# First gated units by row tile, fewer warm-up products, another order of loads, projections and reads back, in a fused spectral filter and gated feed-forward kernel

## The chip, the cores and the metric

One core of one Trainium2 chip. The time is the device time of one execution in microseconds (us); lower is better. TensorE (PE) multiplies, VectorE (DVE), ScalarE (ACT) and GpSimd (POOL) do the rest, SyncE (SP) issues most of the transfers. PEld is TensorE's weight load, which runs beside its products.

## The reference

x has 2048 rows of 512 numbers in bf16. Each row is normalised, and two branches of the result are added to x:

```python
xn = layernorm(x)                     # rows of 512, eps 1e-5
A  = irfft2(rfft2(xn) * (w_r + 1j*w_i))   # over 2048 x 512, w: 2048 x 257
g  = xn @ w_gate                      # 512 x 1792
u  = xn @ w_up                        # 512 x 1792
B  = (gelu_tanh(g) * u) @ w_down      # 1792 x 512
out = x + A + B
```

## The kernel before

The 2048 rows are 16 row tiles j of 128 rows, four of which make a block b (512 rows). Branch B is cut into units. A gated unit `geglu_unit(b, fc, a, w)` makes 128 of the 1792 hidden columns (fc is 0 to 13) for w of a block's 512 rows: four accumulating products with the gate weights into one PSUM bank, four with the up weights into another (both at line 543), gelu on ACT (L555) from the gate bank, and the product of gelu and up on DVE (L563), which frees the up bank. A projection `down_unit(b, n)` multiplies row tile n of a block with w_down in 14 products (L589), and DVE adds the result to x (L600). Row tiles have to be normalised on DVE (`ln_stats`, L411 and L412, and `ln_apply`, L434) and transposed on TensorE before branch B can use them. The inverse root of the variance comes from ACT and DVE for the first two tiles (`ln_sqrt`, `ln_recip`), from POOL for all others (`ln_rstd`).

Branch A is a two-dimensional transform cut into stages of small products: folds on POOL and DVE, `unit_A` (L616) and `unit_d` (L642) for each of 16 tiles, a shuffle through DRAM (`stage_p`), then 16 steps of `unit_B` (L691), the product with the filter on DVE (`product`) and `unit_c` (L722), whose results go to DRAM (`stage_g`, L731) and come back in another order with `back(part, pq, engine)` (L739), and last `unit_e` (L753) and `unit_fin` (L774), whose results POOL adds to x. Each of the four parts that `back` reads holds the results of four steps, in two transfers pq. `unit_B`'s result also crosses partitions through a small transfer (JX).

There is no scheduler: every engine runs its instructions in the order in which the Python code records them, with semaphore waits put in front of an instruction where it depends on another engine or on a transfer. The order is written by hand. At the start, row tiles 0 and 1 are normalised and transposed together (`transposes_by_tile`) while TensorE runs products of zeros (`warm_up`, L524; `NWARM`, of which the last 4 wait for the inverse root). Then come gated units of block 0 on the first 256 rows, fc from 0 to `NHALF`, with the statistics of tiles 2 and 3 behind the first transposes on DVE, and the same units on the other 256 rows. The rest of branch B, whole units on 512 rows, is one list of fillers; `filler(n)` takes the next n of them, and the stages of branch A call it in fixed places. At the end 15 fillers stand between `unit_e` steps, and 3 behind them.

The loads stand in SP's queue in the order of the code, but for the identity and the first up piece, which ACT issues. The weights come in five pieces of columns, `WPIECES`, the first of 384 columns (fc 0 to 2), the second of 256 (fc 3 and 4), the third of 256 (fc 5 and 6). One semaphore per piece counts gate and up together, so the first unit of a piece waits for both. PSUM has eight banks: the units at the start use six of them in turn (`ring_first`, three units), the fillers three (`ring_gu`), the projections of blocks 0 to 2 one (`ring_dn`).

Of the kernel before, what the change touches and what calls it, by code (L numbers as in the profile page):

```python
# [7 lines left out]
ACT = mybir.ActivationFunctionType  # L8
# [6 lines left out]
HD = 256  # L15
NK = 257
FF = 1792
P = 128
NJ = 16
NG = 32  # L20
NDC = 4
NFC = 14
NGG = 3
NX1 = 4
NWARM = (46, 4)
LN_EPS = 1e-5


# [123 lines left out]
class _Sched:  # L152
# [14 lines left out]
    def total(self, stream):  # L167
        return (stream, self.stream_cnt[stream])
# [59 lines left out]
def bass_parallel_sum__spectral_gfnet__glu_gated_geglu__prompt_kernel(  # L228
# [15 lines left out]
    xv = A_x.rearrange("b (p j) d -> p (b j) d", j=NJ)  # L244
# [3 lines left out]
    sch = _Sched()  # L248

    with ExitStack() as es:  # L250
# [4 lines left out]
        x_sb = sb("x_sb", [P, NJ, D])  # L255
# [63 lines left out]
        def sp_bank_bf(slot):  # L319
            return ps_bf[:, slot * 1024:(slot + 1) * 1024]  # L320
# [7 lines left out]
        ring_tr = _Ring((3, 4), bank_readers)  # L328

        streams = [("pe", 1), ("act", 1), ("dve", 1), ("pool", 1)]  # L330
        streams += [(n, 16) for n in ("x0", "x1", "x2", "x3", "xc1", "xc2", "xc3", "ident", "small", "fa", "eg", "wd", "wr", "wi",
                                      "w0", "w1", "w2", "w3", "w4", "dr0", "dr1", "perm1", "jx0", "jx1", "jx2", "jx3", "vd0_0", "vd0_1", "vd0_2", "vd1_0", "vd1_1", "vd1_2", "vd2_0", "vd2_1", "vd2_2", "vd3_0", "vd3_1", "vd3_2", "perm2", "tr2", "tr3", "out")]
        for name, inc in streams:
            sem = es.enter_context(nc.semaphore("sem_" + name))
            sch.add_stream(name, sem, inc)
# [2 lines left out]
        def load(stream, dst, src, eng="sp"):  # L338
            sch.op(eng, lambda e: e.dma_start(dst, src), stream=stream)
            return total(stream)  # L340
# [4 lines left out]
        ev_w = {}  # L345
        spec = {}

        def load_w(i, which=(0, 1), eng="sp"):
            a, b = WPIECES[i]
            for q in which:  # L350
                dst, src = ((wg_sb, B_w_gate), (wu_sb, B_w_up))[q]
                load("w%d" % i, dst[:, :, a:b], src[:, a:b].rearrange("(r p) f -> p r f", p=P), eng=eng)
            ev_w[i] = total("w%d" % i)

        def load_xc(m):
            ev = load("xc%d" % m, x_sb[:, 4 * m:4 * m + 4, :], xv[:, 4 * m:4 * m + 4, :])
# [1 line left out]
                ev_x[j] = ev  # L358

        ev_x = {}  # L360
        load_w(0, (1,), eng="act")
        for j in range(4):
            ev_x[j] = load("x%d" % j, x_sb[:, j, :], xv[:, j, :])
            if j == 1:
                load_w(0, (0,))
        load_w(1)
        load_w(2)
        load_xc(1)
        load_w(3)
# [40 lines left out]
        def ln_stats(j):  # L410
            ev = sch.op("dve", lambda e: e.bn_stats(st[:, j, :], x_sb[:, j, :]), deps=[ev_x[j]])  # L411
            ev_ag[j] = sch.op("dve", lambda e: e.bn_aggr(ag[:, j, :], st[:, j, :]), deps=[ev])  # L412
# [3 lines left out]
        def ln_sqrt(a, b):  # L416
            return sch.op("act", lambda e: e.activation(rstd[:, a:b], ag[:, a:b, 1], ACT.Sqrt, bias=eps_t[:], scale=1.0),
                          deps=[ev_ag[b - 1], ev_eps])

        def ln_recip(a, b, ev):  # L420
            ev = sch.op("dve", lambda e: e.reciprocal(rstd[:, a:b], rstd[:, a:b]), deps=[ev])
            for j in range(a, b):
                ev_rstd[j] = ev
# [9 lines left out]
        def ln_apply(j):  # L433
            ev_xn[j] = sch.op("dve", lambda e: e.tensor_scalar(xn[:, j, :], x_sb[:, j, :], ag[:, j, 0:1], rstd[:, j:j + 1],  # L434
                                                             ALU.subtract, ALU.mult), deps=[ev_rstd[j], ev_ag[j]])

        ev_xnT = {}

        def transposes_by_tile(a, b, ring):

            n = (b - a) * P
            slots = [ring.alloc(1) for _ in range(NDC)]
            banks = [sp_bank_bf(slot)[:, 0:n] for slot, _ in slots]
            evs = []
            for j in range(a, b):
                for r in range(NDC):
                    ev_t = sch.op("pe", lambda e, j=j, r=r: e.transpose(banks[r][:, (j - a) * P:(j - a + 1) * P], xn[:, j, r * P:(r + 1) * P], ident),
                                  deps=[ev_id, ev_xn[j]] + slots[r][1])
                    if j < b - 1:
                        continue  # L450
                    dst = xnT[:, r, a * P:b * P]
                    if r % 2 == 0:
                        ev = sch.op("dve", lambda e, dst=dst, r=r: e.tensor_copy(dst, banks[r]), deps=[ev_t])  # L453
                    else:
                        ev = sch.op("act", lambda e, dst=dst, r=r: e.activation(dst, banks[r], ACT.Copy), deps=[ev_t])
                    ring.add_reader(slots[r][0], ev)
                    evs.append(ev)
            for j in range(a, b):
                ev_xnT[j] = evs

        def transposes(a, b, ring, per=2):

# [66 lines left out]
        def geglu_unit(b, fc, a=0, w=512, ring=None):  # L529

            k = geg["k"]
            geg["k"] = k + 1
            s2 = k % NGG
            hb = b % 2
            ring = ring or ring_gu
            evw = [ev_w[i] for i, (lo, hi) in enumerate(WPIECES) if lo < (fc + 1) * P and fc * P < hi]
            evx = [ev_xnT[4 * b + i] for i in range(a // P, (a + w) // P)]
            gslot, gdeps = ring.alloc(1)

            def mm(e, wsb, slot, dcs=range(NDC)):  # L540
                ins = None
                for dc in dcs:
                    ins = e.matmul(gu_bank(slot)[:, 0:w], wsb[:, dc, fc * P:(fc + 1) * P], xnT[:, dc, b * 512 + a:b * 512 + a + w],  # L543
                                   start=(dc == 0), stop=(dc == NDC - 1))
                return ins

            if b == 0 and fc == 0 and a == 0:
                for dc in range(NDC):
                    ev_gm = sch.op("pe", lambda e, dc=dc: mm(e, wg_sb, gslot, (dc,)), deps=evw + [x[dc] for x in evx] + gdeps)
            else:  # L550
                ev_gm = sch.op("pe", lambda e: mm(e, wg_sb, gslot), deps=evw + evx + gdeps)
            uslot, udeps = ring.alloc(1)
            ev_um = sch.op("pe", lambda e: mm(e, wu_sb, uslot), deps=udeps)
            gg = gg_sb[s2][:, 0:w]
            ev_gg = sch.op("act", lambda e: e.activation(gg, gu_bank(gslot)[:, 0:w], ACT.Gelu_apprx_tanh),  # L555
                           deps=[ev_gm] + gg_readers[s2])
            gg_readers[s2] = []
            ring.add_reader(gslot, ev_gg)
            hdeps = []
            if fc == 0 and a == 0:  # L560
                hdeps = list(hT_readers[hb])
                hT_readers[hb] = []
            ev_h = sch.op("dve", lambda e: e.tensor_tensor(hT[hb][:, fc, a:a + w], gu_bank(uslot)[:, 0:w], gg, ALU.mult),  # L563
                          deps=[ev_um, ev_gg] + hdeps)
            ring.add_reader(uslot, ev_h)
            gg_readers[s2].append(ev_h)
            ev_h_block.setdefault(b, []).append(ev_h)
# [227 lines left out]
            finished(j, ev_o)  # L795


        NHALF = 6
        ln_stats(0)
        ln_stats(1)  # L800
        ev_sq = ln_sqrt(0, 2)
        sch.op("act", lambda e: e.activation(warm[:], eps_t[:], ACT.Gelu_apprx_tanh), deps=[ev_eps])
        ln_recip(0, 2, ev_sq)
        for n, ev in zip(NWARM, (None, ev_rstd[0])):
            warm_up(n, ev)
        ln_apply(0)
        ln_apply(1)
        transposes_by_tile(0, 2, ring_sp)
        ln_stats(2)
        ln_stats(3)  # L810
        ln_rstd(2, 4)
        for fc in range(NHALF):
            geglu_unit(0, fc, 0, 256, ring_first)
            if fc == 1:
                ln_apply(2)
                ln_apply(3)
                half_fold(0)
            if fc == 3:
                transposes(2, 4, ring_tr)
        for fc in range(NHALF):  # L820
            geglu_unit(0, fc, 256, 256, ring_first)
# [6 lines left out]
        for b in range(4):  # L828
            units = [("g", b, fc) for fc in range(NHALF if b == 0 else 0, NFC)]
            if b >= 1:  # L830
                for n, at in enumerate((4, 7, 10, 13) if b < 3 else (3, 5, 7, 14)):
                    units.insert(at + n, ("d", b - 1, n))
            fillers += units
        fillers += [("d", 3, n) for n in range(4)]
# [47 lines left out]
            negate(i)  # L882
        filler(2)
        for u in range(19):
            for v in ((14, 15) if u == 18 else (u - 4,)):
                if v >= 0:
                    unit_c(v)
            if u < 16:
                unit_B(u)
            for v in {15: (12, 13), 16: (14,), 17: (15,), 18: ()}.get(u, (u - 3,)):  # L890
                if v >= 0:
                    product(v)
            if 1 <= u < 18:
                filler()

            if u in (9, 10, 13, 14, 17, 18):
                back(u // 4 - 2, (u - 9) % 4, "act")
        for pq in range(2):
            back(3, pq, "sp")
        filler(todo["left"] - 15 - 3)  # L900
# [59 lines left out]
```

## Time and profile before

| what | value |
|---|---|
| runs | 179.92, 180.50, 180.56 us (median 180.50) |
| the profiled execution | 180.17 us, of which its span is 178.4 |
| busy: PE, DVE, ACT, POOL | 174.7, 116.0, 86.5, 55.2 us |
| PE products, gated units (L543) / projections (L589) | 117.1 / 50.7 us |
| PE's first product of zeros / first transposes / first gated product | 0.97 / 6.22 / 7.14 us |
| PE's last product ends, DVE adds it | 176.2 us, 0.29 us |
| granted TensorE clock | 1.00 in the whole span |

Busy time is a sum over all stages; each row of a timeline is: start, duration, engine, line, operation, tiles, count and, in brackets, the idle time before it and what ended that. In the chain of waits the columns are start, duration and what the chain ran through. The span is from the first to the last instruction of the program; the time has some 1.8 us more around it.

### The profile page before, as it was taken

How to read it: one execution, taken by the hardware profiler on the slowest of the kernel's cores; microseconds unless marked ns; L12 is line 12 of the kernel's file. 1: busy time of each engine (PE TensorE's matmuls, PEld its weight loads, DVE VectorE, ACT ScalarE, POOL GpSimd, SP SyncE). 2: the span in 40 equal slices, each digit the busy share in tenths (PEclk: the TensorE clock that was granted, in tenths of full speed). 3: DMA queues.
4: the chain of work that ended last, by engine and by line, in shares of the span. 5: the costliest groups of instructions: out<-in, count | busy, mean ns of one | idle time of the engine just before them, and what ended most of it. 6: DMA issues, size and time to landing. Idle time of an engine off the chain costs nothing.

```text
span 178.4 us, 3133 instructions
## 1 busy us (share of the span) xinstructions
PE 174.7 (98%) x1136; PEld 98.2 (55%) x1136; DVE 116.0 (65%) x250; ACT 86.5 (49%) x159; POOL 55.2 (31%) x54
## 2 busy tenths in 40 slices
PE   7999999999999999999999999999999999999994
PEld 7888465555555544454555555444455555555443
DVE  3768958798685628438586785954355868885731
ACT  2644357777362633066375764632173536662100
POOL 0073290373630000000000000000017869997760
PEclk9999999999999999999999999999999999999999
DMA  4999999999998693913435666744500111111101
GB/s 147 323 342 379 372 379 149 202 156 239 221 159 198 150 313 106 324 53 81 123 104 125 123 184 149 177 90 117 118 6 29 59 59 32 61 65 48 41 29 59
DMA packets 37520, 27.15 MB, mean 152 GB/s; under 512 B 6656, under 2 KB 36736, under 8 KB 37376
## 3 DMA queue, kind: packets, MB, share of 16 engines
q1 hardware_dynamic: 33664, 24.95, 55.1%
q10 hardware_dynamic: 3840, 2.00, 5.8%
q8 instruction: 9, 0.15, 0.4%
q14 instruction: 7, 0.06, 0.2%
HBM read 17.48 MB, written 6.30 MB: 133 GB/s over the span
## 4 chain that ended last, share of the span: by engine, by line
PE 87%; POOL 5%; DVE 5%; issue 1%
PE ps L543 48%; PE ps L589 25%; POOL bufC L504 5%; PE ps L524 3%; PE ps L722 2%; PE ps L753 2%; PE ps L774 2%; PE ps L691 2%; DVE bufA L434 2%; DVE hT L563 1%; PE ps L616 1%; PE ps L642 1%; PE ps L473 1%; DVE bufB L509 1%; POOL rstd L427 1%
## 5 line engine op out<-in xcount | busy, mean ns | idle before, releaser
L543 PE MATMUL ps<-xnT,wg_sb 128*128 128x512 bf16 (+1 forms) x248 | 58.5, 359 | 0.3 <-DVE xnT L453 0.3
L543 PE MATMUL ps<-xnT,wu_sb 128*128 128x512 bf16 (+1 forms) x248 | 58.6, 359 | 0.0
L563 DVE TENSOR_TENSOR hT<-ps,gg 128x512 bf16<-128x512 f32 (+1 forms) x62 | 39.3, 637 | 23.2 <-PE ps L543 21.6
L589 PE MATMUL ps<-wd_sb,hT 128*128 128x512 bf16 (+2 forms) x238 | 50.7, 367 | 0.0
L555 ACT ACTIVATE gg<-ps 128x512 bf16<-128x512 f32 (+1 forms) x62 | 34.4, 555 | 25.2 <-PE ps L543 23.6
L788 POOL TENSOR_TENSOR bufC<-bufC 128x256 bf16<-128x256 f32 x16 | 14.7, 919 | 86.5 <-DVE bufC L785 86.5
L543 PEld LDWEIGHTS ps<-xnT,wu_sb 128*128 128x128 bf16 x248 | 24.2, 98 | 24.2
L589 PEld LDWEIGHTS ps<-wd_sb,hT 128*128 128x128 bf16 x238 | 22.4, 98 | 23.2
L543 PEld LDWEIGHTS ps<-xnT,wg_sb 128*128 128x128 bf16 x248 | 23.0, 98 | 15.4 <-issue 0.5
L600 DVE TENSOR_TENSOR x_sb<-ps,x_sb 128x512 bf16<-128x512 f32 (+2 forms) x17 | 11.2, 660 | 23.9 <-PE ps L589 23.9
L792 POOL TENSOR_TENSOR x_sb<-x_sb,bufC 128x512 bf16<-128x512 bf16 x16 | 18.7, 1169 | 2.3
L504 POOL TENSOR_TENSOR bufC<-bufA 128x1024 bf16<-128x1024 bf16 x8 | 16.8, 2124 | 7.9 <-DVE bufA L434 7.9
L758 ACT ACTIVATE bufA<-ps 128x512 bf16<-128x512 f32 x16 | 9.4, 597 | 16.9 <-PE ps L753 16.9
L727 ACT ACTIVATE Vp<-ps 128x514 bf16<-128x514 f32 x16 | 9.5, 599 | 15.4 <-PE ps L722 15.4
L650 ACT ACTIVATE bufB<-ps 128x512 bf16<-128x512 f32 x16 | 11.9, 743 | 9.5 <-PE ps L642 9.5
L411 DVE BATCH_NORM_STATS2 st<-x_sb 128x6 f32<-128x512 bf16 x16 | 10.9, 678 | 2.2 <-DMA x_sb<-in_A_x_dram 2.2
L784 DVE TENSOR_TENSOR bufC<-bufC,ps 128x256 f32<-128x256 f32 x16 | 6.7, 421 | 5.3 <-ACT bufC L781 5.3
L696 ACT ACTIVATE Xc<-ps 128x514 bf16<-128x514 f32 x12 | 7.0, 595 | 1.0 <-PE ps L691 1.0
L623 ACT ACTIVATE tmp<-ps 128x512 bf16<-128x512 f32 x9 | 5.4, 597 | 4.4 <-PE ps L616 4.4
L426 POOL TENSOR_SCALAR rstd<-ag 128x4 f32<-128x4 f32 (+1 forms) x4 | 1.3, 316 | 19.9 <-DVE ag L412 19.9
L781 ACT ACTIVATE bufC<-ps 128x256 f32<-128x256 f32 x16 | 6.0, 378 | 2.6 <-PE ps L774 2.6
L788 DVE TENSOR_TENSOR bufC<-bufC 128x256 bf16<-128x256 f32 x16 | 6.8, 425 | 0.5
(50 smaller groups left out, 138.0 us busy)
## 6 DMA issues: line engine op xcount, KB each, us to landing
stage_g<-Vp SPq DMA_DIRECT2D x16, 128.5 KB, 3.1
bufC<-stage_p SPq DMA_DIRECT2D x4, 512.0 KB, 5.5
out_dram<-x_sb SPq DMA_DIRECT2D x15, 128.0 KB, 1.8
wd_sb<-in_B_w_down_dram SPq DMA_DIRECT2D x1, 1792.0 KB, 14.8
stage_p<-bufB SPq DMA_DIRECT2D x7, 256.0 KB, 5.6
wr_sb<-in_A_w_r_dram SPq DMA_DIRECT2D x6, 257.0 KB, 10.8
wi_sb<-in_A_w_i_dram SPq DMA_DIRECT2D x6, 257.0 KB, 10.0
JX<-Xc SPq DMA_DIRECT2D x24, 64.2 KB, 2.3
```

The lines of the kernel that those rows point to most:

```text
L411: ev = sch.op("dve", lambda e: e.bn_stats(st[:, j, :], x_sb[:, j, :]), deps=[ev_x[j]])
L504: ev_hf[m] = [sch.op("pool", lambda e, t=t, op=op: e.tensor_tensor(half[:, m, t, :, :], rows[:, 0, :, :], rows[:, 1, :, :], op), deps=deps ...
L543: ins = e.matmul(gu_bank(slot)[:, 0:w], wsb[:, dc, fc * P:(fc + 1) * P], xnT[:, dc, b * 512 + a:b * 512 + a + w], start=(dc == 0), stop=(d ...
L555: ev_gg = sch.op("act", lambda e: e.activation(gg, gu_bank(gslot)[:, 0:w], ACT.Gelu_apprx_tanh), deps=[ev_gm] + gg_readers[s2])
L563: ev_h = sch.op("dve", lambda e: e.tensor_tensor(hT[hb][:, fc, a:a + w], gu_bank(uslot)[:, 0:w], gg, ALU.mult), deps=[ev_um, ev_gg] + hdeps)
L589: ins = e.matmul(bank(slot)[:, 0:w], hT[hb][:, fc, jj * P:(jj + 1) * P], wd_sb[:, fc, cs], start=(fc == 0), stop=(fc == NFC - 1))
L600: ev_a = sch.op("dve", lambda e, slot=slot, cs=cs, w=w: e.tensor_tensor(x_sb[:, j, cs], bank(slot)[:, 0:w], x_sb[:, j, cs], ALU.add), deps ...
L650: ev_T[j] = sch.op("act", lambda e: e.activation(dst, src, ACT.Copy), deps=[ev_p])
L727: ev_v = sch.op("act", lambda e: e.activation(Vp[sv][:], sp_pair(slot), ACT.Copy), deps=[ev_p] + Vp_readers[sv])
L758: ev_ZT[j] = sch.op("act", lambda e: e.activation(ZT[:, :, j, :], src, ACT.Copy), deps=[ev_p] + [ev_xnT[i][0] for i in (11, 15)])
L788: y = [sch.op(("dve", "pool")[h], lambda e, h=h, op=op: e.tensor_tensor(rS[s2][:, h * HD:(h + 1) * HD], yeS[s2][:, 0, :], yeS[s2][:, 1, :] ...
L792: ev_o = sch.op("pool", lambda e: e.tensor_tensor(x_sb[:, j, :], x_sb[:, j, :], rS[s2], ALU.add), deps=[a, b, ev_xn[j]] + ev_acc.get(j, []))
```

## The change

- `NWARM` goes from (46, 4) to (38, 4).
- Gate and up of each weight piece have semaphores of their own, and the up products wait for theirs.
- SP's queue: x's tiles 0 and 1, first gate piece, second gate piece, tile 2, second up piece, tile 3. Before it was tiles 0 and 1, first gate piece, tiles 2 and 3, second gate piece, second up piece.
- Tiles 0 and 1 have a square root and a reciprocal each. Tile 0 is transposed alone, with its copies out of PSUM on DVE (`transpose_first`); the units fc 0 to 2 (`NQUARTER`) run on 128 rows of tile 0, with tile 1's transposes (copies on ACT) and tile 2's statistics behind the first of them; tile 3's statistics follow; then the same three units run on tile 1. From fc 3 on units are 256 rows wide as before.
- `NHALF` goes from 6 to 7, so the list of fillers is one unit shorter. Each place that takes a filler takes what the next place took before; in front of `unit_e` 4 are left where there were 5. The 15 between `unit_e` steps and the 3 at the end remain.
- The projections of block 2 stand among block 3's units at (1, 2, 7, 14), before at (3, 5, 7, 14). In front of `unit_e` come now unit, projection, unit, projection; before four units and one projection.
- `back` for parts 0 to 2 stands at the start of steps 10, 11, 14, 15 and twice at 17; before at the end of steps 9, 10, 13, 14, 17 and 18.

```diff
-NWARM = (46, 4)
+NWARM = (38, 4)
...
+                name = "w%d%s" % (i, "gu"[q])
+                load(name, dst[:, :, a:b], src[:, a:b].rearrange("(r p) f -> p r f", p=P), eng=eng)
+                ev_w[i, q] = total(name)
...
         load_w(0, (1,), eng="act")
-        for j in range(4):
-            ev_x[j] = load("x%d" % j, x_sb[:, j, :], xv[:, j, :])
-            if j == 1:
-                load_w(0, (0,))
-        load_w(1)
+        load_x(0)
+        load_x(1)
+        load_w(0, (0,))
+        for q in range(2):
+            load_w(1, (q,))
+            load_x(2 + q)
         load_w(2)
...
+        def transpose_first(j, eng):
+            evs = []
+            for h in range(2):
+                slot, bdeps = ring_tr.alloc(1)
...
+                ev_t = sch.op("pe", f_tr, deps=[ev_id, ev_xn[j]] + bdeps)
...
+                evs += [ev, ev]
+            ev_xnT[j] = evs
...
-            ev_um = sch.op("pe", lambda e: mm(e, wu_sb, uslot), deps=udeps)
+            ev_um = sch.op("pe", lambda e: mm(e, wu_sb, uslot), deps=evw_up + udeps)
...
-        NHALF = 6
+        NQUARTER, NHALF = 3, 7
         ln_stats(0)
         ln_stats(1)
-        ev_sq = ln_sqrt(0, 2)
+        ev_sq = [ln_sqrt(j, j + 1) for j in range(2)]
...
-        ln_recip(0, 2, ev_sq)
+        ln_recip(0, 1, ev_sq[0])
         for n, ev in zip(NWARM, (None, ev_rstd[0])):
             warm_up(n, ev)
         ln_apply(0)
+        ln_recip(1, 2, ev_sq[1])
+        transpose_first(0, "dve")
         ln_apply(1)
-        transposes_by_tile(0, 2, ring_sp)
-        ln_stats(2)
+        for fc in range(NQUARTER):
+            geglu_unit(0, fc, 0, P, ring_first)
+            if fc == 0:
+                transpose_first(1, "act")
+                ln_stats(2)
         ln_stats(3)
+        for fc in range(NQUARTER):
+            geglu_unit(0, fc, P, P, ring_first)
         ln_rstd(2, 4)
-        for fc in range(NHALF):
+        for fc in range(NQUARTER, NHALF):
             geglu_unit(0, fc, 0, 256, ring_first)
...
-                for n, at in enumerate((4, 7, 10, 13) if b < 3 else (3, 5, 7, 14)):
+                for n, at in enumerate((4, 7, 10, 13) if b < 3 else (1, 2, 7, 14)):
...
         for u in range(19):
+            for pq in {10: (0,), 11: (1,), 14: (0,), 15: (1,), 17: (0, 1)}.get(u, ()):
+                back((u - 9) // 4 if u < 17 else 2, pq, "act")
...
-            if u in (9, 10, 13, 14, 17, 18):
-                back(u // 4 - 2, (u - 9) % 4, "act")
```

More of the change, by code (lines that the diff above doesn't have):

```diff
@@ L330, in bass_parallel_sum__spectral_gfnet__glu_gated_geglu__prompt_kernel @@
         streams = [("pe", 1), ("act", 1), ("dve", 1), ("pool", 1)]
+        streams += [("w%d%s" % (i, q), 16) for i in range(5) for q in "gu"]
         streams += [(n, 16) for n in ("x0", "x1", "x2", "x3", "xc1", "xc2", "xc3", "ident", "small", "fa", "eg", "wd", "wr", "wi",
-                                      "w0", "w1", "w2", "w3", "w4", "dr0", "dr1", "perm1", "jx0", "jx1", "jx2", "jx3", "vd0_0", "vd0_1", "vd0_2", "vd1_0", "vd1_1", "vd1_2", "vd2_0", "vd2_1", "vd2_2", "vd3_0", "vd3_1", "vd3_2", "perm2", "tr2", "tr3", "out")]
+                                      "dr0", "dr1", "perm1", "jx0", "jx1", "jx2", "jx3", "vd0_0", "vd0_1", "vd0_2", "vd1_0", "vd1_1", "vd1_2", "vd2_0", "vd2_1", "vd2_2", "vd3_0", "vd3_1", "vd3_2", "perm2", "tr2", "tr3", "out")]
         for name, inc in streams:
@@ L351, in load_w @@
                 dst, src = ((wg_sb, B_w_gate), (wu_sb, B_w_up))[q]
-                load("w%d" % i, dst[:, :, a:b], src[:, a:b].rearrange("(r p) f -> p r f", p=P), eng=eng)
-            ev_w[i] = total("w%d" % i)
+                name = "w%d%s" % (i, "gu"[q])
+                load(name, dst[:, :, a:b], src[:, a:b].rearrange("(r p) f -> p r f", p=P), eng=eng)
+                ev_w[i, q] = total(name)
         def load_xc(m):
@@ L360, in bass_parallel_sum__spectral_gfnet__glu_gated_geglu__prompt_kernel, with load_x @@
         ev_x = {}
+        def load_x(j):
+            ev_x[j] = load("x%d" % j, x_sb[:, j, :], xv[:, j, :])
         load_w(0, (1,), eng="act")
-        for j in range(4):
-            ev_x[j] = load("x%d" % j, x_sb[:, j, :], xv[:, j, :])
-            if j == 1:
-                load_w(0, (0,))
-        load_w(1)
+        load_x(0)
[4 more added lines that the diff above has]
+            load_x(2 + q)
         load_w(2)
@@ L437, in bass_parallel_sum__spectral_gfnet__glu_gated_geglu__prompt_kernel, with f_tr @@
         ev_xnT = {}
[L439 to L443, printed above, removed]
+        def transpose_first(j, eng):
             evs = []
[L445 to L459, printed above, removed]
+            for h in range(2):
+                slot, bdeps = ring_tr.alloc(1)
+                bank = sp_bank_bf(slot)[:, 0:HD].rearrange("p (r s) -> p r s", r=2)
+                def f_tr(e, h=h, bank=bank):
+                    ins = None
+                    for r in range(2):
+                        ins = e.transpose(bank[:, r, :], xn[:, j, (2 * h + r) * P:(2 * h + r + 1) * P], ident)
+                    return ins
+                ev_t = sch.op("pe", f_tr, deps=[ev_id, ev_xn[j]] + bdeps)
+                dst, src = xnT[:, 2 * h:2 * h + 2, j * P:(j + 1) * P], bank
+                if eng == "dve":
+                    ev = sch.op("dve", lambda e, dst=dst, src=src: e.tensor_copy(dst, src), deps=[ev_t])
+                else:
+                    ev = sch.op("act", lambda e, dst=dst, src=src: e.activation(dst, src, ACT.Copy), deps=[ev_t])
+                ring_tr.add_reader(slot, ev)
+                evs += [ev, ev]
+            ev_xnT[j] = evs
         def transposes(a, b, ring, per=2):
@@ L535, in geglu_unit @@
             ring = ring or ring_gu
-            evw = [ev_w[i] for i, (lo, hi) in enumerate(WPIECES) if lo < (fc + 1) * P and fc * P < hi]
+            pieces = [i for i, (lo, hi) in enumerate(WPIECES) if lo < (fc + 1) * P and fc * P < hi]
+            evw, evw_up = ([ev_w[i, q] for i in pieces] for q in range(2))
             evx = [ev_xnT[4 * b + i] for i in range(a // P, (a + w) // P)]
@@ L806, in bass_parallel_sum__spectral_gfnet__glu_gated_geglu__prompt_kernel @@
         ln_apply(0)
+        ln_recip(1, 2, ev_sq[1])
+        transpose_first(0, "dve")
         ln_apply(1)
-        transposes_by_tile(0, 2, ring_sp)
-        ln_stats(2)
+        for fc in range(NQUARTER):
[3 more added lines that the diff above has]
+                ln_stats(2)
         ln_stats(3)
+        for fc in range(NQUARTER):
+            geglu_unit(0, fc, P, P, ring_first)
         ln_rstd(2, 4)
-        for fc in range(NHALF):
+        for fc in range(NQUARTER, NHALF):
             geglu_unit(0, fc, 0, 256, ring_first)
-            if fc == 1:
+            if fc == NQUARTER:
                 ln_apply(2)
@@ L817, in bass_parallel_sum__spectral_gfnet__glu_gated_geglu__prompt_kernel @@
                 half_fold(0)
-            if fc == 3:
+            if fc == NHALF - 2:
                 transposes(2, 4, ring_tr)
```

## The prediction

> **What bounds the kernel now.** I read the page's table of engines first, then TensorE's waits, then the start of the timeline, the landings of the first loads, and the chain of waits at three places where work is handed over.
>
> The table of engines, from the page:
>
> ```profile
> PE 174.7 (98%) x1136; PEld 98.2 (55%) x1136; DVE 116.0 (65%) x250; ACT 86.5 (49%) x159; POOL 55.2 (31%) x54
> ```
>
> The waits of TensorE (total, times, longest):
>
> ```profile
> PE ps L524 <- DVE hT L405: 1.0, 1, 1.0
> PE ps L543 <- DVE xnT L453: 0.3, 1, 0.3
> ```
>
> TensorE is busy 174.7 of 178.4 us and the wait list has two entries, both before 7.2 us. So the change can only pay at the start, in the few small gaps below, or by adding work. The start, from the timeline:
>
> ```profile
> 4.89 0.29 ACT L417 ACTIVATE rstd<-ag,eps_t 128x2 f32<-128x2 f32 x1 [1.86 <-DVE ag L412]
> 5.42 0.73 DVE L434 TENSOR_SCALAR bufA<-x_sb,ag,rstd 128x512 bf16<-128x512 bf16 x2
> 6.22 0.61 PE L447 MATMUL ps<-small,bufA 128*128 128x128 bf16 x8
> 6.70 0.49 DVE L453 COPY xnT<-ps 128x256 bf16<-128x256 bf16 x2 [0.55 <-PE ps L447]
> 7.14 0.62 PE L543 MATMUL ps<-xnT,wg_sb 128*128 128x256 bf16 x4 [0.31 <-DVE xnT L453]
> ```
>
> Both row tiles are normalised, then transposed, then multiplied; the first product starts at 7.14 us. From there TensorE runs on. The landings, from the DMA view in narrow windows (the last number is us from issue; issued at 1.64, 2.11 and 3.13 us):
>
> ```profile
> wg_sb<-in_B_w_gate_dram SPq DMA_DIRECT2D x1, 384.0 KB, 4.8
> x_sb<-in_A_x_dram SPq DMA_DIRECT2D x1, 128.0 KB, 4.7
> wg_sb<-in_B_w_gate_dram SPq DMA_DIRECT2D x1, 256.0 KB, 5.0
> ```
>
> The first gate piece lands at 6.44 us, x's third tile at 6.81, the second gate piece at 8.13: SP's queue lands in order, and 256 KB take some 0.9 us. The chain of waits, three places:
>
> ```profile
> 0.97 5.41 PE ps L524 x50
> ...
> 23.55 0.89 PE ps L473 x16
> ...
> 52.75 0.61 DVE bufB L509
> 53.40 0.40 PE ps L616 x4
> ```
>
> The 50 zero products fill 0.97 to 6.2 us; sixteen 128-wide transposes take 0.89, 56 ns each; at 53.2 to 53.4 unit_A(8) waits 0.24 us for a fold. And before the last stage:
>
> ```profile
> 118.20 0.45 PE ps L722 x4
> 118.65 6.91 PE ps L543 x32
> 125.56 3.02 PE ps L589 x14
> 128.58 0.04 issue
> 128.63 0.62 PE ps L753 x8
> ```
>
> Between the last unit_c (done 118.65) and the first unit_e (128.63) lie four gated units (1.73 each) and one projection (3.02), 9.93 us, and the last transfer into V lands just then: 0.04 us of waiting.
>
> **The change part by part.**
>
> *The start.* With one square root per tile, tile 0's can run after its own statistics (about 4.1 us), but the reciprocal stands on DVE behind tile 1's statistics, which end at 4.85. Reciprocal 0.17 and apply 0.41 then end at 5.48 (before: 5.83 and 6.15). The 42 zeros at 107 ns (5.41 us for 50, the first 48 at that pitch) end at 5.47, so they no longer hold the transposes back; at 46 + 4 they did, until 6.2. The four transposes of tile 0 start at 5.51; at the zeros' pitch the first pair is through at 5.93, its copy (0.29) ends at 6.26, and the product followed such a copy by 0.14 before: 6.40. The gate piece, unmoved in its queue, lands at 6.44. I take 6.48 for the first product: 0.66 earlier. Tile 1's four transposes, which stood before 7.14, now stand on TensorE between products: +0.22. Six units on 128 columns are 48 products at 56 ns in place of 24 on 256 columns, whose groups of four start 0.437 apart in the timeline (109 ns each): 2.67 against 2.62, +0.05.
>
> That pitch can be doubted. The Trainium skill ("TensorE: Matmul & The Clock Gate", Back-to-back issue gap) gives about 81 ns per 128-wide matmul when each has its own weight load; by it this term would be an estimated +1.2 us. The row above, sixteen with a weight load each at 56 ns, speaks against it.
>
> *Statistics and loads between the products.* x's tiles 2 and 3 now stand behind the second gate and up pieces. The four together landed by 9.0 and still do; in the new order I put them at 7.35 (gate), 7.7 (tile 2), 8.6 (up), 9.0 (tile 3). DVE waits in order for both tiles, with the products gg times up of later units queued behind: those free the PSUM banks. Statistics take 0.68 + 0.18. With tile 2 at 7.7, unit 1's product on DVE ends near 8.8; unit 4 needs its bank for the up matmuls at 8.72: a wait of 0.15. With tile 3 at 9.0, statistics end at 9.88 and unit 3's product at 10.1; the up matmuls of the first 256-wide unit come to its bank at 9.98: 0.13. Tile 1's copies, now both on ACT (0.38 each), end at 7.9 and its first product is due at 8.05: nothing. Together +0.28; ends 0 (DVE faster than I chain it) and +0.9 (one statistics pair, wholly in the way). rstd for tiles 2 and 3 follows 1.2 us later (POOL 0.23 + 0.73), apply ends near 11.9, and the transposes that need it now come at 12.3, behind two more units: covered by 0.4. The extra waits for the up pieces (8.6 against a need at 9.98) are covered by 1.4 us.
>
> *NHALF 6 to 7.* A unit done in two halves of 0.87 costs what a whole one does, 1.73: nothing. But the list of fillers is one shorter, so each filler slot holds what the next one held. Block 1's first projection (3.02) now stands before unit_A(8) in place of a gated unit (1.73): the 0.24 there goes, -0.24 (ends -0.24 and 0). Between unit_d(15) and unit_B(0) the cover falls from 12.96 to 11.67, but unit_d(15) itself comes later by the same 1.29, behind a projection; its stage writes landed at 68.92 and the shuffle at 75.34 against unit_B's 76.58. I count nothing; without that cover 0.3.
>
> *back() and the projections in turn.* For parts 0 and 1 the end of one step is the start of the next: same place. But the filler ahead of each is now a gated unit where it was a projection, so the pairs stand some 2 us apart, not 4, and run beside JX's small transfers (2.0 us when alone, up to 4.9 beside such a pair in this trace). DVE could wait for JX, and unit_c for DVE: +0.1, ends 0 and +0.5. Part 2 is issued on ACT before unit_c(13) in place of after unit_c(13) and (15). ACT's wait there has the copy of unit_c(13) queued behind it, but the projection at step 16 gives 3.02 us of cover. The second of these transfers used to run beside the last stage writes, which took 4.4 to 4.9 us (median 3.1); it is now gone by then, and I let those land 0.7 earlier. The cover falls from 9.93 to 2 x 1.73 + 2 x 3.02 = 9.50, so unit_e would not wait: -0.04 (ends -0.04 and +0.5). The last three projections stand where they did, and the tail behind 176.2 is untouched.
>
> Sum: -0.66 + 0.22 + 0.05 + 0.28 - 0.24 + 0.10 - 0.04 = -0.29 us. The profiled execution took 180.17 (span 178.38); the runs have 179.92, 180.50 and 180.56. The profiled one lies within them, and 0.3 below their median; against the mean of the four, 180.29, the sum gives 180.0.
>
> **The rivals.**
>
> *The clock (slower).* The zeros' pitch drops from 107 to 56 ns at 6.1 us, 5.2 us after the first matmul, although the granted clock reads 1.00 throughout. Fewer zeros leave TensorE idle from about 6.0 to 6.48, just where that change fell. If a gap of half a microsecond there makes the count begin again at 6.48, up to 5.2 us of products run at half speed: +2.6, less the 0.3 of DVE waits that it swallows; half such a stretch gives +1.0. 181.0 to 182.3. It decides if the fast pitch comes later than about 8.3 us. For it: nothing in this trace shows a gap survived before the change of pitch. Against: the old kernel had a fully busy stretch of five microseconds, and the new one has five behind it too before the gap.
>
> The Trainium skill (same page, The HAM clock gate) has the half clock released after a busy window of about 3.4 us whose phase is free; the 5.2 us of the trace fit a first window that was caught in part. By it the release would lie anywhere from 4.4 to 7.8 us, costing up to an estimated 0.65 where it is late, and it would spread the runs of both kernels.
>
> *unit_e waits.* If the last stage writes gain nothing, the transfers land 9.93 us after unit_c(15), and the cover is 9.50: +0.5 against my sum, 180.5.
>
> *DVE is late at the start.* If tile 3's statistics (0.86) stand wholly ahead of a bank that TensorE wants, the wait is 0.9 where I count 0.28: +0.6, 180.6. For it speaks that DVE is at 2.32 of 2.80 us between 7.2 and 10 already; against it, that six banks hold three units.
>
> *A cheap start.* No DVE wait at all, and the projections in the B stage remove the two gaps before unit_c that the trace has (0.14 and 0.10): -0.5 against the sum, 179.5.
>
> *128-wide products at 81 ns or so.* From the rows I can only bound it: with the 98 ns that a weight load is shown to take, 48 x 0.042 = +2.0; 182.0.
>
> **How the numbers follow.** Forecast 0.56 (179.6 to 180.5 with its unknown terms), unit_e 0.11, DVE late 0.10, cheap start 0.12, the clock 0.08, the pitch 0.03. The measurement can tell about 0.5%, 0.9 us. Against a median of 180.5, faster needs under 179.6: the cheap start and a little of the forecast's lower edge, 0.17. Slower needs over 181.4: most of the clock, the pitch, and late DVE with unit_e waiting, 0.12. The rest, 0.71, is no change that can be told. The range leaves out most of the clock, the pitch and the outermost tails: 179.4 to 181.2.
>
> **What would show it.** First product at 6.4 to 6.6 us; transposes of tile 1 at about 7.0; 128-wide units of 0.45 us each; a wait on TensorE for DVE near 8.7 and 10.0, 0.3 together; no gap before unit_A(8); the last stage writes under 4 us and unit_e without a wait. I am wrong if the first product starts after 7 us, if eight 128-wide products take 0.6 or more, if the 107 ns pitch is still there at 8 us, or if a wait over 0.5 us stands before unit_c, unit_e or unit_B.

## The result, and the profile after

The changed kernel takes 179.83 us (median), the old one 180.63: a ratio of 0.9955, 95% interval 0.9941 to 0.9968, or -0.8 us (-1.1 to -0.6). The prediction was 180.0, in the range 179.4 to 181.2, with no change that can be told as the likeliest; the sum behind it was -0.29. That 180.0 came within 0.2 us of the time is in part luck: the sum was 0.5 us too small, and the time of the old kernel from which it counts, 180.29, was 0.3 too low. The 0.45% lie just within the 0.5% named there, though 18 runs of the old kernel and 17 of the changed one tell them from nothing. One execution of the changed kernel took 1044.69 us, with TensorE at about a sixth of its pace throughout; it is left out, and the trace below is of another execution (179.79 us, span 178.0).

Engines, from the page of the changed kernel:

```profile
PE 173.7 (98%) x1160; PEld 98.6 (55%) x1160; DVE 116.4 (65%) x255; ACT 87.4 (49%) x164; POOL 55.1 (31%) x54
```

TensorE has 24 instructions more and is busy 1.0 us less, since zeros went and half-wide work takes the same time. Its waits (total, times, longest):

```profile
PE ps L532 <- DVE hT L412: 1.0, 1, 1.0
PE ps L532 <- DVE rstd L428: 0.6, 1, 0.6
PE ps L552 <- DVE xnT L462: 0.4, 1, 0.4
```

Still all at the start; the last four zeros now wait for the inverse root. The timeline there (start, duration, engine, line):

```profile
5.46 0.13 DVE L428 RECIPROCAL rstd<-rstd 128x1 f32<-128x1 f32 x1
5.62 0.41 DVE L441 TENSOR_SCALAR bufA<-x_sb,ag,rstd 128x512 bf16<-128x512 bf16 x1
6.18 0.38 PE L456 MATMUL ps<-small,bufA 128*128 128x128 bf16 x4
6.49 0.49 DVE L462 COPY xnT<-ps 128x256 bf16<-128x256 bf16 x2 [0.39 <-PE ps L456]
6.93 0.40 PE L552 MATMUL ps<-xnT,wg_sb 128*128 128x128 bf16 x4 [0.36 <-DVE xnT L462]
7.16 0.39 PE L552 MATMUL ps<-xnT,wu_sb 128*128 128x128 bf16 x4
7.39 0.39 PE L456 MATMUL ps<-small,bufA 128*128 128x128 bf16 x4
```

One tile goes through, the first product starts at 6.93 us, and tile 1's transposes stand behind the first unit. Groups of four 128-wide products start 0.22 to 0.23 apart, 56 ns each. In this execution x's first tile landed at 3.81 us, 0.7 later than in the trace of before, so the chain is late as a whole; the gate piece (issued at 1.64) landed at 6.54, and the last two stage writes took 3.6 us (the DMA view in narrow windows):

```profile
wg_sb<-in_B_w_gate_dram SPq DMA_DIRECT2D x1, 384.0 KB, 4.9
...
stage_g<-Vp SPq DMA_DIRECT2D x2, 128.5 KB, 3.6
```

The one new wait behind the start, from the timeline:

```profile
9.26 0.69 DVE L418 BATCH_NORM_STATS2 st<-x_sb 128x6 f32<-128x512 bf16 x1
9.84 0.60 PE L552 MATMUL ps<-xnT,wg_sb 128*128 128x256 bf16 x4
9.99 0.18 DVE L419 BATCH_NORM_AGGREGATE ag<-st 128x2 f32<-128x6 f32 x1
10.09 0.67 DVE L572 TENSOR_TENSOR hT<-ps,gg 128x128 bf16<-128x128 f32 x3
10.51 0.60 PE L552 MATMUL ps<-xnT,wu_sb 128*128 128x256 bf16 x4
```

The up products at 10.51 should have started 0.44 after 9.84, at 10.28; the bank came free when DVE, done with tile 3's statistics, ran the product at 10.09. That is 0.23 us. The chain of waits before unit_A(8) and before unit_e:

```profile
51.40 1.73 PE ps L552 x8
53.13 0.22 PE ps L625 x4
...
119.82 0.45 PE ps L731 x4
120.26 1.73 PE ps L552 x8
121.99 3.02 PE ps L598 x14
125.01 1.73 PE ps L552 x8
126.74 3.02 PE ps L598 x14
129.76 0.45 PE ps L762 x8
```

No DVE stands before unit_A any more, and from the last unit_c to unit_e TensorE runs through; the last transfer into V had landed at 129.34, 0.26 us before unit_e's first product (129.60).

### The profile page after: what moved, and what is told of

Its sections match the earlier page's. It is cut to its first block, busy times and chain, and to the rows that moved or that the text cites. A ratio compares the mean times of both kernels' runs of the same rounds, so it can differ in the third digit from the quotient of the medians.

```text
span 1042.9 us, 3201 instructions
## 1 busy us (share of the span) xinstructions
PE 1039.7 (100%) x1160; PEld 361.9 (35%) x1160; DVE 120.9 (12%) x255; ACT 92.9 (9%) x164; POOL 55.8 (5%) x54
## 4 chain that ended last, share of the span: by engine, by line
PE 100%; DVE 0%; issue 0%
PE ps L552 57%; PE ps L598 28%; PE ps L700 2%; PE ps L731 2%; PE ps L762 2%; PE ps L625 2%; PE ps L651 2%; PE ps L783 2%; PE ps L532 1%; PE ps L481 1%; PE ps L456 0%; DVE x_sb L609 0%; DVE hT L412 0%
## 5 line engine op out<-in xcount | busy, mean ns | idle before, releaser
L552 PE MATMUL ps<-xnT,wu_sb 128*128 128x512 bf16 (+2 forms) x264 | 321.1, 1506 | 0.0
L552 PE MATMUL ps<-xnT,wg_sb 128*128 128x512 bf16 (+2 forms) x264 | 320.5, 1504 | 0.0
L598 PE MATMUL ps<-wd_sb,hT 128*128 128x512 bf16 (+2 forms) x238 | 301.8, 1630 | 0.0
L552 PEld LDWEIGHTS ps<-xnT,wu_sb 128*128 128x128 bf16 x264 | 86.5, 330 | 209.8 <-issue 208.2
L598 PEld LDWEIGHTS ps<-wd_sb,hT 128*128 128x128 bf16 x238 | 77.2, 327 | 202.1 <-issue 201.5
L552 PEld LDWEIGHTS ps<-xnT,wg_sb 128*128 128x128 bf16 x264 | 81.4, 313 | 141.3 <-issue 137.0
L572 DVE TENSOR_TENSOR hT<-ps,gg 128x512 bf16<-128x512 f32 (+2 forms) x66 | 40.3, 611 | 575.5 <-PE ps L552 575.5
L564 ACT ACTIVATE gg<-ps 128x512 bf16<-128x512 f32 (+2 forms) x66 | 35.1, 532 | 377.1 <-PE ps L552 377.1
L625 PEld LDWEIGHTS ps<-fa,bufB 128*128 128x128 bf16 x64 | 19.9, 327 | 33.1 <-issue 32.1
L762 PEld LDWEIGHTS ps<-fa,bufB 128*128 128x128 bf16 x64 | 19.3, 316 | 31.7 <-issue 30.1
L625 PE MATMUL ps<-fa,bufB 128*128 128x128 bf16 x64 | 27.3, 721 | 0.0
L762 PE MATMUL ps<-fa,bufB 128*128 128x128 bf16 x64 | 27.0, 715 | 0.0
L731 PEld LDWEIGHTS ps<-tmp,small 128*128 128x128 bf16 x32 | 10.2, 320 | 30.8 <-issue 30.8
```

Source lines behind the costliest of these rows:

```text
L598: ins = e.matmul(bank(slot)[:, 0:w], hT[hb][:, fc, jj * P:(jj + 1) * P], wd_sb[:, fc, cs], start=(fc == 0), stop=(fc == NFC - 1))
L625: ins = e.matmul(sp_bank(slot)[:, r * P:(r + 1) * P], fold[:, r // 2, r % 2, j, :], AM[:, j, :], start=True, stop=True)
L731: ins = e.matmul(sp_bank(slot + i)[:, 0:NK], CM[:, kind, :], M1[s2][:, i, :], start=True, stop=True)
L762: ins = e.matmul(sp_bank(slot)[:, ci * P:(ci + 1) * P], V[:, j, V0[ci]:V0[ci] + HD - 1:2], EM[:, j, :], start=True, stop=True)
```

## The experiments

Each time is a median of runs on one chip beside runs of the old kernel there. The ratio after it, with a 95% interval in brackets, is against those runs, and is not simply the quotient of the two medians.

**e0_after: the changed kernel again, whose trace is the one above.**

> The changed kernel again, for an undisturbed trace. All theories: ratio about 0.9955. The sum on record: first product at 6.48 us, TensorE waits for DVE near 8.7 and 10.0 (0.3 together), no gap before unit_A(8), the last stage writes under 4 us, unit_e without a wait. It gives -0.29 us; the runs already gave about -0.8. Theory 'hand-over': the old kernel's margin at unit_e was 0.04 us in the profiled execution and negative in most others, so most runs of before wait there, and the other 0.5 us are those waits; then the changed kernel shows a margin of 0.5 us or more at unit_e. Theory 'start': DVE waits absent and the first product earlier than 6.4; the gain lies before 15 us. Theory 'clock': the fast pitch comes at another time than the first product, and the spread of the runs is the phase of that.

179.83 against 180.72: 0.9955 (0.9939 to 0.9971). The wait at 10.2 us, unit_A(8), the last stage writes and unit_e came as the sum has them; the wait near 8.7 did not come, and the first product came at 6.93 and not 6.48. The margin at unit_e is 0.26, not the 0.5 of 'hand-over'.

**e4_before_again: the old kernel once more, for a second trace.**

> The old kernel unchanged, for a second trace of it and as a control. Ratio 1.000. Theory 'landing': the first loads land at different times from execution to execution (x's first tile at 3.1 or 3.7 to 3.8 us in the traces so far), and the old start, which waits for both tiles and all eight transposes, follows them: first product 7.1 to 7.2 with the early landing, 7.7 to 7.9 with the late one. At unit_e TensorE waits 0.2 us, as steps between matmul starts show (424 ns where 216 is the pitch), at unit_A(8) 0.24, before two unit_c 0.13 and 0.10.

Ratio 1.0003 (0.9988 to 1.0018). The timeline of the start, then the chain before unit_e:

```profile
6.31 0.73 DVE L434 TENSOR_SCALAR bufA<-x_sb,ag,rstd 128x512 bf16<-128x512 bf16 x2
6.87 0.63 PE L447 MATMUL ps<-small,bufA 128*128 128x128 bf16 x8
7.81 0.67 PE L543 MATMUL ps<-xnT,wg_sb 128*128 128x256 bf16 x4 [0.31 <-DVE xnT L453]
```

```profile
120.26 4.52 DMA stage_g<-Vp
124.78 0.02 issue
124.80 0.33 SPq L739
125.12 0.04 issue
125.17 4.19 DMA bufB<-stage_g
129.35 0.05 issue
129.40 0.62 PE ps L753 x8
```

x's first tile landed at 4.02 and the first product started at 7.81, 0.67 later than in the first trace. And the chain goes through the transfers: unit_e waits for them. The last product ahead of it started 0.52 us before it, with a pitch of 0.216: 0.30 lost. In the first trace the same step was 0.42, 0.21 lost, where the chain shows 0.04: a 512-wide product is recorded with 0.38 us where the next can start after 0.22, and these 0.16 us cover the front of a gap. The gaps of 0.24 before unit_A(8) and 0.13 and 0.12 before two unit_c are there again.

**e1_start: the start alone.**

```diff
-        NQUARTER, NHALF = 3, 7
+        NQUARTER, NHALF = 3, 6     # and old projections, old back()
```

> The start alone (row tiles, 42 zeros, loads, semaphores), with NHALF 6, the old projections and the old back(). The sum on record: -0.11 us (0.9994). 'Start': -0.5 to -0.8 (0.996). 'Hand-over': -0.1 to -0.3, and the spread of the runs stays as wide as before's; unit_e waits in its trace, as the hand-over comes earlier by nothing. 'Clock': -0.5 or more, with a narrower spread.

180.77 against 180.72: 1.0016 (0.9998 to 1.0033), no gain, and none of the theories has it; the sum's 0.9994 lies just outside. Its trace is of an execution of 182.14 us, the slowest of twelve, and shows something else, the clock rival (timeline):

```profile
5.56 0.58 PE L456 MATMUL ps<-small,bufA 128*128 128x128 bf16 x4
6.88 0.61 PE L552 MATMUL ps<-xnT,wg_sb 128*128 128x128 bf16 x4 [0.73 <-DMA wg_sb<-in_B_w_gate_dram]
...
9.84 0.63 PE L552 MATMUL ps<-xnT,wg_sb 128*128 128x128 bf16 x4
10.27 0.43 PE L552 MATMUL ps<-xnT,wu_sb 128*128 128x128 bf16 x4
10.54 0.39 PE L552 MATMUL ps<-xnT,wg_sb 128*128 128x128 bf16 x4
```

After 0.9 us without a product (the gate piece landed at 6.83), groups of four stand 0.43 apart, half pitch, up to 10.4 us. With NHALF 6, moreover, the transposes of tiles 2 and 3 come one unit sooner and wait 0.5 us for DVE in this trace: the start needs NHALF 7 beside it, which the sum had as a cover. The old kernel with a first product as early as 7.16 loses as much at these transposes (0.53 in e3). At unit_e e1's trace loses 0.24.

**e6_nhalf: NHALF 7 alone.**

```diff
-        NHALF = 6
+        NHALF = 7
```

> NHALF 7 alone on the old kernel. Expected: the gap before unit_A(8) goes (-0.24) and one of the gaps before unit_c (-0.10), but four fillers ahead of unit_e with the old order are three units and one projection, 8.2 us, where the transfers need about 10.0 from the end of the last unit_c: TensorE waits some 1.8 us there, 1.5 more than before. Net +1.2 us (1.0065). A theory by which the shorter list is free of cost gives -0.3.

181.63 against 180.52: 1.0069 (1.0049 to 1.0088), +1.25 us, the expected sum from other parts. The gap before unit_A(8) is gone; 1.13 us are lost at unit_e, where 1.8 were expected, and 0.48 between the last two unit_c, where none was.

**e2_back and e3_projections: back() alone, projections alone.**

```diff
 e2
         for u in range(19):
+            for pq in {10: (0,), 11: (1,), 14: (0,), 15: (1,), 17: (0, 1)}.get(u, ()):
+                back((u - 9) // 4 if u < 17 else 2, pq, "act")
...
-            if u in (9, 10, 13, 14, 17, 18):
-                back(u // 4 - 2, (u - 9) % 4, "act")
 e3
-                for n, at in enumerate((4, 7, 10, 13) if b < 3 else (3, 5, 7, 14)):
+                for n, at in enumerate((4, 7, 10, 13) if b < 3 else (1, 2, 7, 14)):
```

> back() alone in its new places, all else as before. The sum on record: last stage writes land 0.7 us sooner, the 0.04 us at unit_e goes, nothing else: same within 0.1 us. 'Hand-over': -0.4 to -0.5 us (0.9975) and a narrower spread, as the runs that wait at unit_e lose their wait. 'Start' and 'clock': 1.000.

> Block 2's projections at (1, 2, 7, 14) alone, NHALF 6: the five fillers ahead of unit_e are then three units and two projections, 11.2 us in place of 9.9, so the margin at unit_e grows by 1.3 us with the transfers as they were. 'Hand-over': -0.4 to -0.5 us (0.9975), as much as e2. The sum on record: -0.04. 'Start' and 'clock': 1.000.

e2: 180.35, 0.9991 (0.9975 to 1.0006). e3: 180.34, 0.9979 (0.9968 to 0.9991), -0.4 us. Projections alone, which lengthen the cover by 1.3 us, take the wait away (0.65 us to spare in its trace). back() alone does not: the transfers of part 2, now together, took up to 5.6 us, the last stage writes 4.3 to 4.6 as before, and unit_e still waited 0.18. So 'hand-over' holds for e3 and not for e2.

**e7_oldback: the changed kernel with back() in its old places.**

```diff
-            for pq in {10: (0,), 11: (1,), 14: (0,), 15: (1,), 17: (0, 1)}.get(u, ()):
-                back((u - 9) // 4 if u < 17 else 2, pq, "act")
...
+            if u in (9, 10, 13, 14, 17, 18):
+                back(u // 4 - 2, (u - 9) % 4, "act")
```

> The changed kernel with back() in its old places. In the changed kernel the last transfers landed 9.35 us after the last unit_c began, against 10.2 in the old one, and unit_e had 0.26 us to spare. If the early issue of part 2 is what shortened that, the need returns to about 10.1 and unit_e waits 0.5 us: +0.5 us (1.003). If the shorter need comes from the units' order alone (a projection at step 16), back() is worth nothing here: 1.000.

180.83 against 180.52: 1.0019 (0.9998 to 1.0041), where the changed kernel is at 0.9955. The chain before unit_e:

```profile
121.70 4.50 DMA stage_g<-Vp
126.19 0.02 issue
...
126.58 4.21 DMA bufB<-stage_g
130.79 0.05 issue
130.83 0.62 PE ps L762 x8
```

The last stage write takes 4.5 us again beside part 2's late transfer, the need is 10.03 us from the last unit_c's start, and unit_e loses 0.47, the last unit_c 0.30. Against e5, the changed kernel with more zeros in the same runs (0.9967), back() is worth 0.9 us here, for 0.5 expected, and alone next to nothing. Why is not shown. Part 2 goes out some 3 us ahead of the last two writes in e2 as in the changed kernel; what differs is how long its second transfer runs beside them. It lands 2.6 us after the first of the two is issued in e2, where that write takes 4.6 us, and 2.0 us after in the changed kernel, where it takes 3.6.

**e5_zeros46: 46 + 4 zeros in the changed kernel.**

```diff
-NWARM = (38, 4)
+NWARM = (46, 4)
```

> The changed kernel with the 46 + 4 zeros of before. If the zeros hold the transposes back at half pitch (the sum on record), the first product comes up to 0.4 us later where the clock is released late, nothing where it is released early: +0.1 to +0.3 us (1.001). Theory 'clock': a gap-free run of zeros up to the transposes releases the clock more surely, runs above 180.5 vanish, and the median stays within 0.1.

179.92, 0.9967 (0.9953 to 0.9981), runs from 179.74 to 180.06: as the changed kernel. In its trace the fast pitch began early enough that all 50 zeros were through by 5.2 us.

**e11_zeros16: 16 + 4 zeros.**

```diff
-NWARM = (38, 4)
+NWARM = (16, 4)
```

> The changed kernel with 16 + 4 zeros: TensorE idle from about 2.7 us to the last four zeros at 5.1, and again up to the first product at 6.9. Theory 'clock' (the rival on record): idle time before the release starts the count anew, the 107 ns pitch lasts to about 10 us, and the products of 3.4 us run at half speed: +1.5 us against the changed kernel (1.004 against before). If gaps do not matter: within 0.1 of the changed kernel.

181.59 against 180.69: 1.0043 (1.0020 to 1.0066), 1.6 us over the changed kernel's ratio. The timeline:

```profile
0.97 1.89 PE L532 MATMUL ps<-hT 128*128 128x128 bf16 x16 [0.97 <-DVE hT L412]
5.83 0.61 PE L532 MATMUL ps<-hT 128*128 128x128 bf16 x4 [2.97 <-DVE rstd L428]
7.21 0.58 PE L552 MATMUL ps<-xnT,wg_sb 128*128 128x128 bf16 x4 [0.26 <-DVE xnT L462]
...
11.01 0.53 PE L552 MATMUL ps<-xnT,wg_sb 128*128 128x128 bf16 x4
11.37 0.39 PE L552 MATMUL ps<-xnT,wu_sb 128*128 128x128 bf16 x4
```

Half pitch from 7.21 to 11.3. The rival's mechanism is real. With 38 zeros one trace, e1's, shows it, and those of after, e7, e9 and e10 do not. This trace also loses 0.50 us at unit_e although back() has its new places: its last transfers landed 10.06 us after the last unit_c began.

**e8_old_start: the old start with all the rest.**

```diff
 before
-        NHALF = 6
+        NHALF = 7      # and new projections, new back()
```

> The old start (both tiles together, 46 + 4 zeros, old loads) with all the rest of the change: NHALF 7, projections at (1, 2, 7, 14), back() in its new places. The sum on record, by which the start is worth 0.11 us: -0.7 against before (0.996). Theory 'landing', by which the old start follows late x tiles and the new one does not: the start is worth 0.3 to 0.5, so -0.3 to -0.5 against before (0.9978), the spread of the runs stays wide, first product 7.1 to 7.9, no gaps before unit_A(8) and unit_e.

180.23 against 180.69: 0.9962 (0.9939 to 0.9984). The rest of the change is worth -0.7 us (-1.1 to -0.3) by the runs; the start the difference to 0.9955, 0.1 us, with intervals that also allow nothing and 0.5. Neither theory is told apart by it. In its trace the first product starts at 7.64, the gap before unit_A(8) is gone, and unit_e loses 0.17.

**e9_stats_later: tile 3's statistics behind tile 1's first unit.**

```diff
-        ln_stats(3)
         for fc in range(NQUARTER):
             geglu_unit(0, fc, P, P, ring_first)
+            if fc == 0:
+                ln_stats(3)
```

> The changed kernel with tile 3's statistics behind the first unit of tile 1 instead of ahead of it. In its trace TensorE lost 0.23 us at 10.2 us on a bank that DVE frees only after those statistics. If DVE's order is the cause, that wait goes: -0.2 us against the changed kernel. If tile 3's late landing (9.24 us) is, DVE waits for it one product later, and the wait moves to the next up products: 0.

179.75, 0.9954 (0.9930 to 0.9978). In its trace the 0.23 at 10.2 us is gone, so DVE's order caused it, not the landing (9.33). The runs do not tell 0.2 us: a wait of 0.17 at 9.0 us and one of 0.24 at unit_e stand in the same trace.

**e10_gate_first: e9, and the first gate piece on ACT's queue, the first up piece on SP's.**

```diff
-        load_w(0, (1,), eng="act")
+        load_w(0, (0,), eng="act")
         load_x(0)
         load_x(1)
-        load_w(0, (0,))
+        load_w(0, (1,))
```

> As e9, with the first gate piece on ACT's queue and the first up piece on SP's, so that the piece that the first product needs lands first (5.2 to 6.4 us in the traces, against 6.4 to 7.2). First product at 6.4 to 6.6 where x's chain allows it; its up products then wait for the piece on SP. If the gate piece bounds the start: -0.2 beyond e9. If x's chain does: as e9.

179.62 against 180.69: 0.9930 (0.9908 to 0.9952), -1.3 us, the fastest kernel here. Beyond e9 that is 0.4 by the ratios, with intervals that overlap, where 0.2 was expected. The chain of the start:

```profile
5.80 0.29 PE ps L456 x2
6.09 0.02 issue
6.11 0.30 DVE xnT L462
6.41 0.14 issue
6.55 0.62 PE ps L552 x8
```

The gate piece landed at 5.82, and the first product starts at 6.55, held by the transposes and their copy alone. Part comes back as a wait of 0.33 us on a bank at 8.8.

## Why the prediction was right, and where its steps were not

**The first product (-0.66).** These are the traces (us; landings of x's tiles 0 and 1 and of the gate piece):

| start | landings | first product |
|---|---|---|
| old: before, e3, e6 | 3.1 to 3.2, 3.8 to 4.1, 6.4 to 7.2 | 7.14, 7.16, 7.44 |
| old: e2, e4, e8 | 3.7 to 4.0, 4.2 to 4.8, 6.6 to 7.0 | 7.83, 7.81, 7.64 |
| new: e1, e5, e9 | 3.1, 3.5 to 4.5, 6.8 | 6.88, 6.83, 6.81 |
| new: after (e0), e11 | 3.8 to 4.0, 4.1 to 4.3, 6.5 to 6.7 | 6.93, 7.21 |
| new: e7 | 3.15, 4.78, 7.18 | 7.22 |

Without e11, which has 16 zeros and transposes at half pitch, the means are 7.50 and 6.94, -0.57. The step that failed was to take one execution's landing for the landing: 6.44 was the earliest gate piece of all. With x early the new start stands 0.05 us behind the gate piece and gains some 0.4 (means 7.25 and 6.84); with x late, where the old start followed the tiles, some 0.8 (7.76, and 6.93 in the one trace). I had worked out that the two limits lay within 0.1 us of each other, but not that each moves by more than that. By the prediction's own sign, a first product after 7 us, e7's execution (7.22) speaks against it.

**Tile 1's transposes and the narrow products (+0.22, +0.05).** As forecast: 0.22 in the chain, and 56 ns a product. By the pitch of 81 ns of the Trainium skill ("TensorE: Matmul & The Clock Gate", Back-to-back issue gap) the 48 products would have taken an estimated 1.2 us more; the trace differs, and decides.

**DVE between the products (+0.28).** 0.23 at 10.2 us where 0.13 was forecast, and nothing near 8.7 in the trace of after (0.17 at 9.0 to 9.4 in those of e5, e7 and e9). The cause was the order of DVE's queue, as worked out, and tile 3 landed at 9.2 where I had 9.0.

**unit_A(8) (-0.24).** Gone in every trace with NHALF 7, as forecast.

**unit_e (-0.04).** Mis-sized by a misread view. The 0.04 us that the chain shows is what is left of a gap behind the recorded end of the matmul before; the steps between matmul starts give 0.21 and 0.30 in the two traces of the old kernel. That the last stage writes land sooner held, though part 2's second transfer was not gone by then, as the prediction has it, but ran 2.0 us beside them: the need fell from 10.2 to 9.35 us after (9.5 to 9.8 in e5 and e9), against a cover of 9.6. The cover is not safe: unit_e loses nothing in after, e5 and e10, but 0.17 in e8, 0.24 in e9 and 0.50 in e11. The rival 'unit_e waits' is what e7 shows without back()'s move, at 0.47 for the 0.5 predicted.

**unit_c (+0.10).** Wrong in sign: one of the two gaps went, -0.10, as with NHALF 7 alone (e6), and none came in the trace of after.

**The sum.** From the first product to the end of the last one the old kernel took 168.99 and 169.09 us, the changed one 168.86 (e5 and e9: 169.09 and 169.06): -0.04, behind a first product that comes 0.57 sooner. Most of that 0.57 is paid back at once, by tile 1's transposes, the narrow products and DVE (0.22, 0.05 and 0.23). A mark that all kernels pass is the first product of unit_A. NHALF 7 puts one gated unit (1.73) ahead of it that comes behind it with NHALF 6, and this is added to the times of the latter here. The mark then comes at 28.20 us in the mean of the six traces of the old start (27.74 to 28.43) and at 28.09 in after, e5, e7 and e9 (27.82 to 28.45). So by the traces the start as a whole is worth 0.1 us, as the sum's first four terms have it (-0.11), though executions differ by more than that; e1's runs (no gain) and e8's (0.1) agree.

Behind that mark, with the same unit taken out, the old kernel took 148.39 and 148.49 us to the end of the last product, the changed one 147.81 (e5 and e9: 147.80 and 148.05), -0.3 to -0.7: unit_A(8) 0.24, unit_c 0.10, unit_e 0.21 to 0.30. There the prediction had -0.18, and the terms that it mis-sized are unit_e and unit_c. Together the traces give some -0.7, against -0.8 (-1.1 to -0.6) by the runs. Runs of the old kernel reach 182 us and no trace shows such a one; e8's runs put -0.7 behind the start, its one trace -0.3. Whether the old hand-over at unit_e waits longer in those runs stays open.

**The clock rival.** Right as a mechanism, with a longer gap than the half microsecond on which it rested: half pitch up to 10.4 us in one trace of the new start, behind 0.94 us without a product, and +1.6 us with 16 zeros. The prediction's price, 1.0 to 2.3, held it. The sign that was named for it, the 107 ns pitch at 8 us, stands in e1 and e11. How many runs it touches is not shown.

## What to carry to other kernels

A kernel whose matrix engine never rests can be bettered only where work changes hands, and there the slack of one execution is not the slack: look at landings in several traces before counting on a cover of 0.1 us. Moves that shift one list against another have to be tried together: alone, NHALF cost 1.25 us here, back() gave almost nothing and the projections 0.4, and the three together 0.7. A gap behind a matmul is read from the starts of two matmuls, since the recorded duration hides its first 0.16 us.

## What the runs showed of the hardware

Up to its release TensorE ran at 107 ns per 128 columns, then at 56, though the granted clock of the page reads 1.00; where the trace has a record of that clock at all, it begins only at the release. The release came at 3.6 to 6.8 us in the traces with 38 or more zeros other than e1 (3.6 in e2 and e5, 4.0 in e8, 4.8 after, 5.2 in e7, 5.8 in e9, 6.1 before, 6.8 in e6), at 10.4 in e1 and 11.3 in e11. A pause of 0.52 us among the zeros did not put it off (e9); one of 0.94 (e1) or of 3 us (e11) did. The Trainium skill ("TensorE: Matmul & The Clock Gate", The HAM clock gate) has a window of about 3.4 us whose phase is free: the spread of the release agrees, and so does e1, where it came 3.5 us after the first product. The 4.4 us that the prediction took from it for the earliest release does not: 3.6 is only 2.7 us after the first product of zeros, so such a window would have begun some 0.7 us ahead of that. These traces would fit a window that may hold 0.5 to 0.7 us of idle time and not 0.9, which no run here tried by itself.

The first 128 KB load, issued at 0.72 us in every trace, landed at 3.1 to 3.2 us in some executions and at 3.7 to 4.0 in others.
